# Three x tiles turned ahead of the key weights and one behind them, where it was two and two

## The chip, the core and the metric

The kernel runs on one core of a Trainium2 chip. The metric is device time in microseconds (us) of one execution, lower is better. A core has a matrix engine (PE, with its weight loads listed apart as PEld), a vector engine (DVE), a scalar engine (ACT), GpSimd (POOL) and SyncE (SP), which in this kernel only issues transfers. The transfers run on 16 DMA engines that all queues share.

## The reference

Two branches read the same input x (2048 tokens by 640, bf16) and are mixed by a gate for each token. In the first, x is multiplied by wqkv (640 by 1920) into queries, keys and values of 32 heads of 20. Queries and keys are multiplied by a small matrix w_phi of each head, and the features are the softmax of the result and the softmax of its negative. The state of a head is the sum over all tokens of (key features times values); an output is (query features times state) over a normaliser, and goes through wo. In the second branch the result is (gelu(x @ w_gate) * (x @ w_up)) @ w_down, with 1728 hidden columns. Cut to its core:

```python
phi_q = concatenate([softmax(q @ w_phi), softmax(-(q @ w_phi))])     # phi_k likewise
num = einsum("bhqf,bhfd->bhqd", phi_q, einsum("bhsf,bhsd->bhfd", phi_k, v))
den = einsum("bhqf,bhf->bhq", phi_q, phi_k.sum over tokens) + 1e-6
a = (num / den) @ wo
b = (gelu(x @ w_gate) * (x @ w_up)) @ w_down
g = sigmoid((x * gate_w).sum(-1))
out = g * a + (1 - g) * b
```

## The kernel before

The 2048 tokens are 16 tiles of 128. PE needs x with its columns on the partitions; that turned copy is `xT`, kept in SBUF for the whole kernel. Tiles 0 to 3 are loaded as they are (line 225) and turned by PE itself (line 331). Tiles 4 to 15 are turned on their way in by DMA transposes, each issued by `xturn(t, n)` (line 233) for n tiles from tile t on. One such DMA has one completion: whoever reads any of its n tiles waits for the whole of it.

Two more DMA transposes, issued by `wload` (line 229), bring the key part and the query part of wqkv in turned form: `wkT` and `wqT`, 640 by 640 each. They are needed because the kernel folds w_phi into the weights once: `fold(kt, "k", banks)` (matmuls on line 374, evictions on lines 383, 385 and 386) multiplies a block of `wkT` with a block-diagonal form of w_phi in a pair of PSUM banks, from where ACT or DVE copies one column of each head (`wref`) and DVE subtracts it from the others and writes the folded weight.

All transfers of the start are issued from SP's one queue, in the order of the code in `loads` (lines 242 to 251): two loads of x, five of the value weights, then the transposes. None of them waits for anything, so SP issues them one after another, and the DMA engines work them off in that order. The order of PE's work is the order of the code in `attention_state` (lines 539 to 612). Nothing is reordered: a helper, `_Sched`, only puts a wait on a semaphore ahead of an operation when something that it reads or overwrites isn't finished yet. Around the change it reads, with the PSUM banks as arguments:

```python
v(4, 6)
v(5, 0)
f(0, "k", (2, 3))
f(1, "k", (4, 5))
f(2, "k", (6, 7))
self.strip(6)
f(3, "k", (0, 1))
self.strip(0)
v(6, 2)
f(4, "k", (4, 5))
v(7, 6)
k(0, 0)
f(0, "q", (2, 3))
```

`v(t, b)` is ten matmuls (line 396, reached through `proj`) that project tile t on the value weights into banks b and b + 1, and an ACT eviction (line 437). It reads `xT` of tile t. `f` is a fold as above, six matmuls; `strip` is a small DVE memset of PSUM. `k` projects a tile on the folded key weights and takes exponentials on ACT (line 453).

After that a loop over the 16 tiles does keys, values, queries and the sum of the state (line 506), then the second branch runs for four blocks of 512 tokens (line 396 again, through `gateup`), and at the end the down projections with the output projection (line 717), their evictions (lines 728 and 730) and the stores.

Of the kernel before, what the change touches and what calls it, by code (L numbers as in the profile page):

```python
# [107 lines left out]
class _Kernel:  # L108
# [108 lines left out]
    def loads(self):  # L217
        sc, nc = self.sc, self.nc
        D, KD, DH, P_ = self.D, self.KD, self.DH, P
        w3 = self.wqkv.rearrange("(kt p) n -> p kt n", p=P)  # L220

        x4 = self.x[0:self.BT, :].rearrange("(p j) n -> p j n", j=self.TB)

        def xload(q, j):
            sc.dma(q, lambda e: e.dma_start(self.xtok[:, j:j + 2, :], x4[:, j:j + 2, :]),  # L225
                   writes=[("xtok", j), ("xtok", j + 1)])

        def wload(T, c0, key):
            sc.dma("sp", lambda e: e.dma_start_transpose(T[:, :, :], self.wqkv[:, c0:c0 + D]), writes=[key])  # L229

        def xturn(t, n):
            a, z = t * P, (t + n) * P
            sc.dma("sp", lambda e: e.dma_start_transpose(self.xT[:, :, a:z], self.x[a:z, :]),  # L233
                   writes=[("xT", k) for k in range(t, t + n)])
        sc.op("pool", lambda e: e.memset(self.gz[:, :], 0.0), writes=["gz"])
        sc.op("act", lambda e: e.activation(self.gtmp[:, 0:1], self.nc.const_aps.tensor(1.0, [P, 1], BF16), AF.Exp),
              writes=["gtmp"])
        sc.op("pool", lambda e: e.memset(self.ident[:, :], 0.0), writes=["ident"])
        sc.op("pool", lambda e: e.affine_select(self.ident[:, :], self.ident[:, :], pattern=[[-1, P]],
                                                compare_op=ALU.not_equal, fill=1.0, base=0, channel_multiplier=1),  # L240
              writes=["ident"])
        xload("sp", 0)
        xload("sp", 2)
        for kt in range(KD):
            sc.dma("sp", lambda e: e.dma_start(self.w3[:, kt, 0:D], w3[:, kt, 2 * D:3 * D]), writes=[("wv", kt)])  # L245
        xturn(4, 2)
        wload(self.wkT, D, "wkT")
        xturn(6, 2)
        wload(self.wqT, 0, "wqT")
        xturn(8, 4)  # L250
        xturn(12, 4)
        def pool(fn, writes, reads=()):
            sc.op("pool", fn, reads=reads, writes=writes)
        for i in range(KD):
            n = self.HHI[i] - self.HLO[i] + 1
            base = P * i - DH * self.HLO[i]
            m = self.mask[:, i, 0:n]
            pool(lambda e, m=m: e.memset(m, 1.0), [("mask", i)])
            pool(lambda e, m=m, n=n, base=base: e.affine_select(
                m, m, pattern=[[-DH, n]], compare_op=ALU.is_ge, fill=0.0, base=base, channel_multiplier=1),  # L260
                [("mask", i)])
            pool(lambda e, m=m, n=n, base=base: e.affine_select(
                m, m, pattern=[[DH, n]], compare_op=ALU.is_ge, fill=0.0, base=DH - 1 - base, channel_multiplier=-1),
                [("mask", i)])
        sc.dma("act", lambda e: e.dma_start(
            self.wphi_sb[:, :, :], self.wphi.rearrange("h d f -> (h d) f").rearrange("(i p) f -> p i f", p=P)),
            reads=[("mask", 1)], writes=["wphi"])
        sc.dma("act", lambda e: e.dma_start(self.gz[0:KD, :], self.gw.rearrange("(k p) -> k p", p=P)), writes=["gz"])
        for r in (0, 1):
            m = self.hmask[:, r, :]  # L270
            pool(lambda e, m=m: e.memset(m, 1.0), [("hmask", r)])
            pool(lambda e, m=m, r=r: e.affine_select(
                m, m, pattern=[[-DH, self.HG]], compare_op=ALU.is_ge, fill=0.0, base=-64 * r,
                channel_multiplier=1), [("hmask", r)])
            pool(lambda e, m=m, r=r: e.affine_select(
                m, m, pattern=[[DH, self.HG]], compare_op=ALU.is_ge, fill=0.0, base=DH - 1 + 64 * r,
                channel_multiplier=-1), [("hmask", r)])
        pool(lambda e: e.tensor_tensor(self.hmask[:, 2, :], self.hmask[:, 0, :], self.hmask[:, 1, :], ALU.add),
             ["hm"], reads=[("hmask", 0), ("hmask", 1)])
        for s in range(self.NSV):  # L280
            pool(lambda e, s=s: e.memset(self.vaug[:, s, :, DH:self.DA], 1.0), [("vone", s)])
        for s in range(self.NSE):
            pool(lambda e, s=s: e.memset(self.consts(self.Ek, s, 0), 1.0), [("Ekc", s)])
            pool(lambda e, s=s: e.memset(self.consts(self.Ek, s, 1), 1.0), [("Ekp", s)])
        for s in range(self.NEQ):
            pool(lambda e, s=s: e.memset(self.consts(self.Eqt, s, 0), 1.0), [("Eqtc", s)])
            pool(lambda e, s=s: e.memset(self.consts(self.Eqt, s, 1), 1.0), [("Eqtp", s)])
# [565 lines left out]
```

## Time and profile before

| | |
|---|---|
| median of 3 runs | 284.77 us (284.77 to 285.49) |
| the profiled execution's own time | 284.86 us |
| its span, first to last instruction | 283.5 us |
| PE busy | 280.3 us, 99% of the span |
| DVE, ACT, POOL busy | 172.8, 104.8, 13.2 us |
| granted clock of PE | 1.00 |
| moved by DMA | 24.11 MB, mean 85 GB/s |

Lines of an engine's order of time read: start, length, engine, line, operation, what is written and what is read, shapes, count, and in brackets the idle time before it with what ended it. "SPq" is SP's issue of a transfer, which ends long before the transfer does; the time from the start of an issue until the data are there is called landing. "q1" is the queue of the kernel's transfers, "q8" the one by which the engines fetch their instructions. GB/s stands in a strip of 40 equal slices of the stretch asked for. L396 is one helper line that serves most of the projections, so its rows are told apart by shape and by time.

### The profile page before, as it was taken

Reading aid. Unit: us, or ns where it says so; the run is one execution under the profiler, and the core shown is the slowest. Engines: PE = TensorE matmul, PEld = TensorE weight load, DVE = VectorE, ACT = ScalarE, POOL = GpSimd, SP = SyncE. Lnnn points to the kernel's source line nnn. Section 1 sums busy time; section 2 is a strip of 40 time slices with the busy share of each in tenths; the row PEclk is TensorE's granted clock in tenths of the full one; section 3 lists DMA queues with packets and bytes.
Section 4 is the critical chain, followed back from the end, with each engine's and each line's share of the span. In section 5 each row is a group of like instructions: output and inputs, shape, how many; then the busy total and the mean of one; then the engine's idle time right before and its main releaser. Section 6 shows DMA issues by size and latency. Waiting matters only on the chain.

```text
span 283.5 us, 6887 instructions
## 1 busy us (share of the span) xinstructions
PE 280.3 (99%) x2922; PEld 174.7 (62%) x2922; DVE 172.8 (61%) x325; ACT 104.8 (37%) x191; POOL 13.2 (5%) x67
## 2 busy tenths in 40 slices
PE   8999999999999999999999999999999999999996
PEld 5677777777754444444444444445777777777786
DVE  1369999999995332667242334325883883884801
ACT  4357888887852223222332223231112112012011
POOL 7500101110000000000000000000000000000000
DMA  8994398989999500011000000000133233232221
GB/s 227 189 219 91 60 198 179 192 180 165 171 250 353 146 0 0 2 23 24 2 0 0 0 2 0 0 0 2 25 50 85 58 44 76 72 44 76 73 73 49
DMA packets 58922, 24.11 MB, mean 85 GB/s; under 512 B 50954, under 2 KB 58378, under 8 KB 58890
## 3 DMA queue, kind: packets, MB, share of 16 engines
q1 hardware_dynamic: 58224, 23.63, 38.8%
q8 instruction: 23, 0.38, 0.6%
q10 hardware_dynamic: 666, 0.03, 0.2%
q14 instruction: 9, 0.07, 0.1%
HBM read 9.04 MB, written 2.62 MB: 41 GB/s over the span
## 4 chain that ended last, share of the span: by engine, by line
PE 94%; SPq 3%; DMA 2%; issue 0%; ACT 0%
PE ps L396 61%; PE ps L717 28%; PE ps L662 2%; DMA xT<-in_A_x_dram 2%; PE ps L506 2%; SPq L229 1%; SPq L245 1%; PE ps L374 1%; SPq L233 1%; SPq L225 0%; ACT outsb L730 0%
## 5 line engine op out<-in xcount | busy, mean ns | idle before, releaser
L396 PE MATMUL ps<-xT,wu_sb 128*128 128x512 bf16 x260 | 64.6, 379 | 0.0
L396 PE MATMUL ps<-xT,wg_sb 128*128 128x512 bf16 x260 | 64.6, 379 | 0.0
L633 ACT ACTIVATE gl<-ps 128x512 bf16<-128x512 f32 x52 | 31.1, 598 | 76.0 <-PE ps L396 73.8
L635 DVE TENSOR_TENSOR hT<-ps,gl 128x512 bf16<-128x512 f32 x39 | 26.7, 691 | 43.2 <-PE ps L396 43.2
L717 PE MATMUL ps<-wd_sb,hT 64*128 64x320 bf16 x648 | 48.4, 296 | 0.0
L396 PEld LDWEIGHTS ps<-xT,wu_sb 128*128 128x128 bf16 x260 | 25.4, 98 | 30.9 <-DVE hT L635 0.4
L396 PEld LDWEIGHTS ps<-xT,wg_sb 128*128 128x128 bf16 x260 | 25.0, 98 | 29.4
L730 ACT ACTIVATE outsb<-ps,Gm 128x320 bf16<-128x320 f32 (+2 forms) x31 | 14.6, 516 | 71.7 <-PE ps L717 71.7
L396 PE MATMUL ps<-w,xT 128*128 128x304 bf16 (+3 forms) x280 | 40.6, 296 | 0.3 <-DMA xT<-in_A_x_dram 0.3
L717 PEld LDWEIGHTS ps<-wd_sb,hT 64*128 64x128 bf16 x648 | 30.9, 94 | 12.2 <-issue 0.4
L396 PEld LDWEIGHTS ps<-w,xT 128*128 128x128 bf16 x280 | 26.4, 97 | 10.2 <-DMA xT<-in_A_x_dram 0.5
L717 PE MATMUL ps<-wo_sb,goT 64*128 64x320 bf16 (+2 forms) x340 | 26.5, 288 | 0.0
L495 DVE TENSOR_TENSOR Ek<-Ek,Dk 128x1320 bf16<-128x1320 bf16 x16 | 24.5, 1532 | 0.5
L688 DVE TENSOR_TENSOR O<-ps,RH 128x640 bf16<-128x640 f32 x32 | 24.8, 817 | 0.0
L486 DVE TENSOR_REDUCE Dk<-Ek 128x66 f32<-128x1320 bf16 x16 | 24.3, 1520 | 0.0
L396 PE MATMUL ps<-wq,xT 128*128 128x304 bf16 x160 | 23.3, 292 | 0.0
L453 ACT ACTIVATE Eqt<-ps 128x627 bf16<-128x627 f32 x32 | 20.5, 694 | 6.5 <-PE ps L396 6.5
L453 ACT ACTIVATE Ek<-ps 128x627 bf16<-128x627 f32 x32 | 20.5, 694 | 2.8 <-PE ps L396 2.6
L635 DVE TENSOR_TENSOR xT<-ps,gl 128x512 bf16<-128x512 f32 x13 | 9.0, 692 | 18.2 <-PE ps L396 18.2
L717 PEld LDWEIGHTS ps<-wo_sb,goT 64*128 64x128 bf16 x340 | 15.9, 94 | 5.3
L396 PEld LDWEIGHTS ps<-wq,xT 128*128 128x128 bf16 x160 | 15.0, 98 | 4.5
L717 PE MATMUL ps<-wd_sb,xT 64*128 64x320 bf16 (+2 forms) x270 | 16.0, 269 | 0.0
(77 smaller groups left out, 180.1 us busy)
## 6 DMA issues: line engine op xcount, KB each, us to landing
out_dram<-outsb SPq DMA_DIRECT2D x7, 320.0 KB, 2.3
wd_sb<-in_B_w_down_dram SPq DMA_DIRECT2D x1, 2080.0 KB, 10.6
wg_sb<-in_B_w_gate_dram SPq DMA_DIRECT2D x5, 224.0 KB, 4.0
wu_sb<-in_B_w_up_dram SPq DMA_DIRECT2D x5, 224.0 KB, 3.4
wg_sb<-in_B_w_gate_dram SPq DMA_DIRECT2D x5, 192.0 KB, 3.7
wu_sb<-in_B_w_up_dram SPq DMA_DIRECT2D x5, 192.0 KB, 3.3
w<-in_A_wqkv_dram SPq DMA_DIRECT2D x5, 160.0 KB, 4.0
wo_sb<-in_A_wo_dram SPq DMA_DIRECT2D x1, 800.0 KB, 9.6
```

What stands on the lines that cost most here:

```text
L229: sc.dma("sp", lambda e: e.dma_start_transpose(T[:, :, :], self.wqkv[:, c0:c0 + D]), writes=[key])
L396: self.sc.op("pe", lambda e: e.matmul(self.ps[:, bank * 512 + c0:bank * 512 + c0 + n], lhs, rhs, start=first, stop=fin), reads=reads, writ ...
L453: self.sc.op("act", lambda e: e.activation(dst, src, AF.Exp, scale=scale), reads=[("ps", b), ("ps", b + 1)], writes=[(name, sl, s)])
L486: self.sc.op("dve", lambda e: e.tensor_reduce(self.Dk[:, se, 0, :].rearrange("p (u h) -> p u h", h=self.HG), self.k_view(se), AX.X, ALU.ad ...
L495: sc.op("dve", lambda e: e.tensor_tensor(v, v, R.rearrange("p (u h) -> p u h", h=self.HG).unsqueeze(3).to_broadcast([P, 2 * self.G, self.H ...
L506: self.sc.op("pe", lambda e: e.matmul(self.bank(b)[:, c:c + n], self.Ek[:, se, g * P:(g + 1) * P], va[:, w * g:w * g + n], start=(t == 0 a ...
L633: sc.op("act", lambda e: e.activation(self.gl[:, slot, :], self.bank(banks[0]), AF.Gelu_apprx_tanh), reads=[("ps", banks[0])], writes=[("g ...
L635: sc.op("dve", lambda e: e.tensor_tensor(hT, self.bank(banks[1]), self.gl[:, slot, :], ALU.mult), reads=[("ps", banks[1]), ("gl", slot)], ...
L662: sc.op("pe", lambda e: e.matmul(self.ps[:, o:o + n], self.Eq[a:a + 64, g, t * P:(t + 1) * P], self.KV[a:a + 64, g, 0:n], start=(g in (0, ...
L688: dve(lambda e, o=o, f=f, s=s: e.tensor_tensor(o, V[s][:, :, 0:DH], f, ALU.mult), rb + [key(6 + s)], [("O", s, sl)], guard=old)
L717: sc.op("pe", lambda e: e.matmul(self.bank(bk, w), lhs, rhs, start=opens and x == 0, stop=end and not opens, skip_group_check=True), reads ...
L730: sc.op("act", lambda e: e.activation(dst, self.bank(bk, w), AF.Copy, scale=g), reads=rd, writes=wr)
```

## The change

The second x transpose gives one of its two tiles to the first. Tile 6 is turned by the DMA that is issued ahead of wkT, together with tiles 4 and 5; tile 7 alone is turned by the DMA between wkT and wqT. Nothing else differs: the number of transfers, the bytes, the order of the other entries in the queue and all instructions of the other engines are as before.

```diff
@@ loads
-        xturn(4, 2)
+        xturn(4, 3)
         wload(self.wkT, D, "wkT")
-        xturn(6, 2)
+        xturn(7, 1)
         wload(self.wqT, 0, "wqT")
         xturn(8, 4)
         xturn(12, 4)
```

## The prediction

> **What bounds the kernel now.** I read the page first, then the chain that ended last, then TensorE's (PE) order of time in the first 20 us, and last the queue of SP and the DMA by stretches. The page and the chain:
>
> ```profile
> span 283.5 us, 6887 instructions
> PE 280.3 (99%) x2922; PEld 174.7 (62%) x2922; DVE 172.8 (61%) x325; ACT 104.8 (37%) x191; POOL 13.2 (5%) x67
> ...
> PE 94%; SPq 3%; DMA 2%; issue 0%; ACT 0%
> ...
> 4.09 1.93 SPq L233
> 6.07 3.70 SPq L229
> 9.81 5.65 DMA xT<-in_A_x_dram
> 15.51 1.54 PE ps L396 x10
> ```
>
> PE is busy in 280.3 of 283.5 us. The chain runs through SP's queue until 9.81, through the transfer that turns tiles 6 and 7 until 15.46, and from 15.51 it is PE alone up to the last eviction. So whatever PE gains or loses near 15 us reaches the end whole, and nothing else here can. PE in that place, in order of time (start, length, idle in brackets):
>
> ```profile
> 11.00 2.90 PE L396 MATMUL ps<-w,xT 128*128 128x345 bf16 x20
> 13.74 1.50 PE L374 MATMUL ps<-BD,wkT 128*128 128x140 bf16 x24
> 15.51 1.54 PE L396 MATMUL ps<-w,xT 128*128 128x345 bf16 x10 [0.27 <-DMA xT<-in_A_x_dram]
> ...
> 13.61 1.44 PEld L374 LDWEIGHTS ps<-BD,wkT 128*128 128x128 bf16 x24
> ...
> 20.45 0.19 DVE L385 COPY wref<-ps 128x32 f32<-128x32 f32 x1 [1.53 <-PE ps L374]
> ```
>
> The first line is v of tiles 4 and 5 (they need the first turn, by the weight load at 10.94), the second the k folds 0 to 3 (they need wkT, from 13.61), the third v of tile 6, which sat 0.27 us for the second turn. These 0.27 us are all of PE's idle time between its start and its end. What SP issues and when it lands:
>
> ```profile
> 4.09 1.93 SPq L233 DMA_TRANSPOSE xT<-in_A_x_dram  x1
> 9.81 1.40 SPq L233 DMA_TRANSPOSE xT<-in_A_x_dram  x1
> 11.26 4.77 SPq L229 DMA_TRANSPOSE wqT<-in_A_wqkv_dram  x1
> ...
> DMA to landing us min/median/max: 4.8/4.8/4.8
> DMA to landing us min/median/max: 6.5/6.5/6.5
> DMA to landing us min/median/max: 7.8/7.8/7.8
> ```
>
> The landings are those of the first turn, of wkT and of wqT: 4.09 + 4.8 = 8.9, 6.07 + 6.5 = 12.6, 11.26 + 7.8 = 19.1. Slack before use: 10.94 - 8.9 = 2.0 for tiles 4 and 5, 13.61 - 12.6 = 1.0 for wkT, 19.74 (first weight load on wqT) - 19.1 = 0.65 for wqT; tile 6 has -0.27. The DMA between 12.8 and 14.6 us:
>
> ```profile
> GB/s 637 267 290 267 256 40 0 0 0 0 0 0 0 0 0 0 0 0 0 0 6 6 6 11 6 11 6 11 6 11 11 6 11 11 6 11 6 17 23 245
> q8 instruction: 1, 0.02, 3.3%
> ```
>
> One fetch of 16 KB of instructions starts there (12.8), and from 13.0 to 14.55 all 16 DMA engines stand nearly still: the second x turn was in flight, and it landed at 15.46 only. The next ones begin at 24.3, 37.1, 49.7 and 62.9, at PE's pace, so the first comes at 12.8 in the changed kernel too, as PE has done the same by then.
>
> **The change part by part.** Instructions on PE, DVE, ACT and POOL are the same in number and order; only two entries of SP's queue change size. The number of DMA issues stays.
>
> First turn, two tiles to three. A tile is 128 x 640 x 2 B = 164 KB. In full flow the DMA moves 288 GB/s (its mean from 14.6 to 17.4 us), so one tile is 0.57 us. Landing 8.9 + 0.57 = 9.5, use at 10.94: hidden, by v of tiles 0 to 3 on PE. SP's issue grows from 1.93 by between 0.2 (a 128-token turn in the output stage issues in 1.20, a 256-token one in 1.40) and 1.0 a tile (512 tokens take 3.45 at the end of this series, (3.45 - 1.40)/2). I take 0.6, the middle, near the DMA's own 0.57.
>
> wkT, moved behind one more tile. It lands 0.2 to 1.0 later by the issue, 0.57 later by the flow: 12.8 to 13.6, taken as 13.15. Use at 13.61: slack 0.45 where it was 1.0, and at the far end of the bound none. Behind it on PE stand all folds and everything else, in order.
>
> Second turn, two tiles to one. It ends as early as before or earlier, since the bytes ahead of it are the same: 15.46 at the latest by the flow. Tile 7 is first wanted when v of tile 6 (10 matmuls, 1.54) and fold 4 (0.32) are done, 17.2: hidden by 1.7 us. SP's issue of it costs 1.20 to 1.40, so wqT's issue begins at 11.0 to 11.9 instead of 11.26; its bytes ahead are the same, so 19.1 is kept, against a use that comes 0.1 sooner (19.6). The later turns (8 to 15) follow wqT and have several us.
>
> Tile 6 then is there at 9.5, and PE's wait of 0.27 goes. What is late next: v of tile 6 writes banks 2 and 3, which fold 0 used; they come free when DVE has evicted them:
>
> ```profile
> 14.55 0.80 DVE L386 TENSOR_TENSOR w<-ps,wref 128x608 bf16<-128x608 f32 x1
> ```
>
> That is 15.35, and with the 0.05 that the chain shows between a release and PE's start, 15.40. So PE starts v of tile 6 at 15.40 and not at 15.24, where the folds ahead of it end: the gain is 15.51 - 15.40 = 0.11, with 0.27 as the upper bound. After that DVE and ACT follow PE: fold 4 and tile 7 need evictions that end at 16.1 and 16.9, before 17.0, and the q folds' evictions start only when PE has written (DVE's line at 20.45 above waits for PE), so they move along.
>
> Sum: 284.86 (the profiled execution: span 283.5 and 1.36 around it) - 0.11 = 284.75, beside a median of 284.77; the profiled execution stands 0.09 above that median.
>
> **The skill against the row.** The Trainium skill's page "DMA: Bandwidth & Descriptors", section "Latency and other measured facts", gives 261 GB/s for DMA transposes whose middle dimension isn't contiguous. By that a tile would take 0.63 instead of 0.57, wkT would land 0.06 later still, and the sum would be the same. The same page's "Queues, rings and completion order" says that an engine's completion write lands only after all its earlier writes, those of other queues among them. By that rule an instruction fetch that is served before wkT's last write on one engine would hold the whole of wkT back, which speaks against the change; the trace shows only the standstill of 1.55 us in an x turn, and no landing of wkT behind a fetch. The sum by that rule would be the first rival's, by the row alone 284.75.
>
> **The rivals.** *The fetch catches wkT (slower).* Before, wkT is in at 12.6, ahead of the fetch at 12.8; after, it is due at 12.8 to 13.6, inside the standstill. If a part of it is still on the way at 13.0, it comes when the DMA moves again, 14.55, or up to 15.46 as the x turn did. PE would idle from 13.74 to W + 0.05, DVE's evictions move with it, and 0.11 is still won: 14.55 gives 0.86 - 0.11 = +0.75, 15.46 gives 1.77 - 0.11 = +1.66: 285.6 to 286.5, middle 286.05. It decides from a landing of 13.8 on. For it: the two times meet. Against: wkT's reads would be done by about 11.15 + 0.57 = 11.7 (in 8.05 to 11.15 the flow is even, then it breaks to 16 GB/s), a full us before the fetch, and only completions would be open.
>
> *wkT a little late.* Landing between 13.7 and 14.5 for the far end of SP's issue or a longer completion: -0.1 to +0.7, some 285.1. wqT shows a tail as long: its reads end at 17.4 and it lands at 19.1, 1.7 later where wkT's tail is 1.4.
>
> *Three tiles in one turn land late.* A 512-token turn takes 6.5 to 7.1 from issue to landing; 4.09 + 7.1 = 11.2 would hold tile 4 by 0.25, and push wkT to 14.8, +1.0: 285.9. Against it: that turn starts behind wqT's tail and holds four tiles.
>
> *Nothing is won.* DVE's eviction or another wait in its place takes all of 0.27: 284.86.
>
> **How the numbers follow.** Chances: the gain of 0.11, 0.43; the fetch catches wkT 0.36; a little late 0.12; three tiles late 0.05; nothing or something else 0.04. A measurement of this kernel can tell about 0.3%, 0.85 us, from no change: the limits are 283.9 and 285.6. Faster than 283.9 isn't to be had from 0.27 us of idle time: 0.03. Slower takes nearly all of the fetch's case (0.35), most of the late tiles (0.03) and a rest: 0.39. Within: 0.58. The likeliest case's own range is 284.5 to 285.2; the range with the rivals is 284.4 to 286.4, which leaves out the tails of both.
>
> **What would show it.** Right: no idle time of PE before v of tile 6 for a DMA, a short one at most for DVE's eviction; wkT's landing from its issue such that the folds start at 13.74 as before; tile 6 landed by 10. Wrong: PE or its weight loads idle before the first fold (L374) with wkT as releaser, and the length of that idle time less 0.1 is then the loss. If DMA stands still elsewhere than at 13.0, the fetch has moved, and the second rival falls. Most likely to make the prediction wrong is the size of wkT's delay: 0.45 us of slack are worked out from a flow, not seen.

## The result and the profile after

The changed kernel takes 286.02 us in the median of 16 runs (285.39 to 287.14), the kernel before 285.23 in 16 runs taken beside them (284.59 to 285.51): a ratio of 1.0031, 95% interval 1.0021 to 1.0041. It is slower by 0.8 us. The profiled execution took 286.26 us, 1.40 more than that of the kernel before. Single executions scatter by about 1 us, so traces are compared with traces and medians with medians.

The page of the changed kernel, and from its chain that ended last (start, length, what) the pieces around the change:

```profile
span 284.9 us, 6886 instructions
PE 280.6 (98%) x2922; PEld 174.5 (61%) x2922; DVE 172.7 (61%) x325; ACT 104.8 (37%) x191; POOL 13.2 (5%) x67
...
PE 94%; DMA 3%; SPq 2%; DVE 0%; issue 0%; ACT 0%; DVEq 0%
```

```profile
4.09 3.09 SPq L233
7.24 7.94 DMA wkT<-in_A_wqkv_dram
15.22 0.50 PE ps L374 x6
16.04 0.81 DVE w L386
16.90 1.54 PE ps L396 x10
```

PE is busy as long as before, so what was lost is idle time. The chain no longer goes through the turn of tile 6 but through wkT: its issue begins at 7.24 where it was 6.07, and it lands 7.94 later, at 15.18, where it was 12.57. PE in order of time:

```profile
11.80 2.91 PE L396 MATMUL ps<-w,xT 128*128 128x345 bf16 x20 [0.55 <-DMA xT<-in_A_x_dram]
15.22 1.43 PE L374 MATMUL ps<-BD,wkT 128*128 128x140 bf16 x24 [0.51 <-DMA wkT<-in_A_wqkv_dram]
16.90 1.54 PE L396 MATMUL ps<-w,xT 128*128 128x345 bf16 x10 [0.24 <-DVE w L386]
```

Three waits stand where there was one. Tiles 4 and 5 wait for the first turn, which takes 7.7 us to land instead of 4.8 (4.09 + 7.7 = 11.8):

```profile
DMA to landing us min/median/max: 7.7/7.7/7.7
```

The folds wait for wkT. Then v of tile 6 waits, no more for a transfer but for DVE's eviction of fold 0. It starts at 16.90 against 15.51, 1.39 later, and this is the whole of the 1.40 us.

Why both transfers are late is seen in the DMA from 8.7 to 12 us (GB/s in 40 slices of 0.0825 us). First the kernel before, then the changed one:

```profile
GB/s 43 270 289 292 292 289 292 285 292 292 289 292 295 279 298 289 292 292 289 292 285 289 295 289 292 289 285 292 295 197 59 25 40 22 59 81 93 112 143 177
```

```profile
GB/s 267 143 68 65 115 99 71 47 47 71 90 130 121 99 304 93 74 96 74 22 19 19 12 0 0 0 9 6 9 9 9 9 9 9 12 34 261 295 292 276
...
q8 instruction: 1, 0.02, 1.8%
```

Before, wkT is read without a break at some 290 GB/s until 11.1, and no instructions are fetched meanwhile; the first fetch starts at 12.8, behind it. After, the flow is thin at the same place, some 50 to 140 GB/s from 8.8 on. At 9.9 the instruction fetch starts (the lone 304), and from 10.3 to 11.6 nearly nothing moves. A transpose reads its data in packets of 256 B, so that counting them tells which transfer is being read: the 1,920 packets of the first turn are read by 8.85, so the thin flow behind it is wkT's own start. wkT's reads end near 14.0 instead of 11.1.

### The profile page after: what moved, and what is told of

Its sections match the earlier page's. It is cut to its first block, busy times and chain, and to the rows that moved or that the text cites. A ratio compares the mean times of both kernels' runs of the same rounds, so it can differ in the third digit from the quotient of the medians.

```text
span 284.9 us, 6886 instructions
## 1 busy us (share of the span) xinstructions
PE 280.6 (98%) x2922; PEld 174.5 (61%) x2922; DVE 172.7 (61%) x325; ACT 104.8 (37%) x191; POOL 13.2 (5%) x67
## 4 chain that ended last, share of the span: by engine, by line
PE 94%; DMA 3%; SPq 2%; DVE 0%; issue 0%; ACT 0%; DVEq 0%
PE ps L396 60%; PE ps L717 28%; DMA wkT<-in_A_wqkv_dram 3%; PE ps L662 2%; PE ps L506 2%; SPq L233 1%; PE ps L374 1%; SPq L245 1%; SPq L225 0%; DVE w L386 0%; ACT outsb L730 0%; DVE wref L385 0%; DVEq L42 0%
## 5 line engine op out<-in xcount | busy, mean ns | idle before, releaser
L730 ACT ACTIVATE outsb<-ps,Gm 128x320 bf16<-128x320 f32 (+2 forms) x31 | 14.6, 516 | 71.8 <-PE ps L717 71.8
L717 PEld LDWEIGHTS ps<-wo_sb,goT 64*128 64x128 bf16 x340 | 15.9, 94 | 5.3
## 6 DMA issues: line engine op xcount, KB each, us to landing
wd_sb<-in_B_w_down_dram SPq DMA_DIRECT2D x1, 2080.0 KB, 11.3
```

What stands on the lines that cost most here:

```text
L717: sc.op("pe", lambda e: e.matmul(self.bank(bk, w), lhs, rhs, start=opens and x == 0, stop=end and not opens, skip_group_check=True), reads ...
L730: sc.op("act", lambda e: e.activation(dst, self.bank(bk, w), AF.Copy, scale=g), reads=rd, writes=wr)
```

## The experiments

Four explanations were held against each other. The *size theory*: a turn of three tiles has a long tail of its own. The *bytes theory*: wkT is late by the 164 KB ahead of it and by no more. The *issue* (or *starvation*) *theory*: SP is held by the longer first turn, wkT's issue begins too late, and its reads run thin. The *fetch theory* was added to the last: PE's instruction fetch, which gets in when the flow is thin, halts the transposes. In the recorded expectations of the first runs it is a part of the issue theory.

### Tiny loads on SP ahead of wkT (e1_sp_delay)

```diff
         xturn(4, 2)
+        for i in range(3):
+            sc.dma("sp", lambda e: e.dma_start(self.tiny[:, i, :], self.gw.rearrange("(p k) -> p k", p=P)), writes=[("tiny", i)])
         wload(self.wkT, D, "wkT")
```

> The kernel before, with three loads of a few bytes on SP's queue between the first turn (tiles 4 and 5) and wkT: each costs SP about 0.43 us of issue, the order and the bytes of all else stay. Issue theory (the third tile hurts because SP is occupied by the first turn for 3.09 us instead of 1.93, so wkT's issue begins at 7.24 instead of 6.07, the DMA engines run out of issued work near 8.7, and an instruction fetch then gets in at 9.9 and halts the transposes): wkT's issue begins near 7.4, the flow of 288 GB/s breaks between 8 and 9.5, the fetch comes near 10 instead of 12.8, wkT lands between 14 and 15.3, PE sits before the first fold for 0.4 to 1.7 us, and the time is 0.5 to 1.6 us above the kernel before. Size theory (a turn of three tiles has a long tail of its own) and bytes theory (wkT is late because 164 KB more stand ahead of it): neither size nor bytes change, wkT lands by 13, the time stays within 0.3 us of the kernel before.

Measured: 286.51 us, ratio 1.0059 (1.0046 to 1.0071). wkT's issue begins at 8.21. The DMA from 8.2 to 10.6 us, and PE's only large wait (line 377 is line 374 of the kernel before):

```profile
GB/s 286 286 294 178 55 42 26 7 2 2 3 2 2 5 7 3 0 0 0 0 0 0 60 85 107 107 128 145 149 158 145 154 196 183 243 222 213 213 128 107
```

```profile
15.49 1.43 PE L377 MATMUL ps<-BD,wkT 128*128 128x140 bf16 x24 [1.54 <-DMA wkT<-in_A_wqkv_dram]
```

No turn has grown, and three times 128 packets of 10 B, under 4 KB in all, are no load: the DMA engines stand mostly idle from 8.5 to 9.5. Yet wkT lands at 8.21 + 7.2 = 15.4. Size and bytes theory both fall as the whole cause: a late issue alone makes the DMA run dry and then run thin. The fetch came at 13.2, not near 10 as expected, and hit the end of wkT: a second place where it does harm. How much of the 1.54 us it makes, and how much the late issue, this run doesn't separate.

### The same tiles ahead of wkT in two transfers (e3_split)

```diff
-        xturn(4, 3)
+        xturn(4, 2)
+        xturn(6, 1)
         wload(self.wkT, D, "wkT")
         xturn(7, 1)
```

> The changed kernel with its first turn in two transfers, tiles 4 and 5, then tile 6, both ahead of wkT. Same bytes in the same order, but no transfer of three tiles. Issue theory: SP needs 1.9 + 1.2 = 3.1 us for the two, wkT's issue begins near 7.3 as in the changed kernel, the flow breaks and the fetch comes near 10; wkT lands between 14 and 15.3; tile 4 no longer waits (landing near 9), so PE sits only before the folds, for 0.4 to 1.7 us: 0.3 to 1.5 us above the kernel before. Size theory: the tail goes with the size, wkT lands by 13.3, the time is 0 to 0.3 us below the kernel before.

Measured: 285.90 us, ratio 1.0033 (1.0020 to 1.0046), as much as the change itself. SP is busy with the two turns from 4.11 to 7.97, and wkT's issue begins at 8.01. PE:

```profile
14.85 1.43 PE L375 MATMUL ps<-BD,wkT 128*128 128x140 bf16 x24 [0.87 <-DMA wkT<-in_A_wqkv_dram]
16.61 1.53 PE L397 MATMUL ps<-w,xT 128*128 128x345 bf16 x10 [0.33 <-DVE w L387]
```

The wait of tile 4 is gone with the long transfer, the wait for wkT is not, and the time doesn't fall. So the size theory explains at most the wait of tile 4, and this wait isn't needed for the loss. What size alone costs wkT the run doesn't price, because its issue begins 0.77 us later than in the changed kernel (8.01 against 7.24).

### All four tiles ahead of wkT (e6_four)

```diff
-        xturn(4, 3)
+        xturn(4, 4)
         wload(self.wkT, D, "wkT")
-        xturn(7, 1)
```

> The changed kernel with tile 7 in the first turn as well: four tiles ahead of wkT, none behind it. Starvation theory: SP's issue of the first turn lasts until the DMA has read all but some 1400 of its 2560 packets, to 8 or later, so wkT's issue begins at 8.2 or later, its reads at 9.5 or later, and it lands between 14 and 16.5: 0.4 to 2.5 us above the kernel before. Bytes theory: wkT is late by the 328 KB that are new ahead of it, 1.14 us at 288 GB/s: it lands at 13.7, and the time is within 0.3 us of the kernel before.

Measured: 286.50 us, ratio 1.0048 (1.0035 to 1.0061). SP's issue of the turn takes 4.49 us, wkT's begins at 8.63 and it lands at 15.7:

```profile
12.22 2.91 PE L395 MATMUL ps<-w,xT 128*128 128x345 bf16 x20 [1.33 <-DMA xT<-in_A_x_dram]
15.73 1.43 PE L373 MATMUL ps<-BD,wkT 128*128 128x140 bf16 x24 [0.60 <-DMA wkT<-in_A_wqkv_dram]
```

The issue grows with every tile (1.9, 3.1, 4.5 us for two, three, four). The loss is 0.48% where the change's is 0.31%, but their intervals overlap, so that it grows is not shown. The bytes theory, within 0.3 us, fails again.

### Value weights issued from ACT (e2_act_loads, and its control e7_before_act)

```diff
-            sc.dma("sp", lambda e: e.dma_start(self.w3[:, kt, 0:D], ...
+            sc.dma("sp" if kt < 3 else "act", lambda e: e.dma_start(self.w3[:, kt, 0:D], ...
```

> The changed kernel (three tiles, then one), with the last two of the five value-weight loads issued from ACT's queue instead of SP's: SP reaches the first turn 0.9 us earlier, its size and the bytes stay. Issue theory: first turn issued from 3.2, wkT from about 6.3, the DMA still has work issued ahead when the first turn is done, the flow holds to the end of wkT, the fetch comes after it, wkT lands by 13.3, tile 4 by 9.8, PE doesn't sit before the folds, and the time is 0.9 to 1.5 us below the changed kernel in its profile, 0 to 0.3 us below the kernel before. Size theory: the tail of the first turn stays (landing at 11 or later), wkT lands at 14 or later, the time stays 0.5 us or more above the kernel before.

> The kernel before with the last two value-weight loads issued from ACT's queue. It is the control for the changed kernel with the same edit: what the edit alone does. Issue theory: SP is 0.9 us ahead, wkT lands at 12.6 or up to 0.5 earlier, the fetch still falls behind wkT into the second turn, tile 6 still waits for it up to 15.4: within 0.3 us of the kernel before. If the value weights themselves come later from ACT's queue, v of tiles 0 to 3 would stretch, and this run shows it: tiles 4 and 5 would start after 11.0.

Measured: 287.40 us, ratio 1.0082 (1.0069 to 1.0096) with three tiles first, 285.92 us, 1.0033 (1.0020 to 1.0045) with two. The edit does harm by itself: loads from two queues share the DMA, the first x tiles come later, and PE starts its transposes 0.7 us (two tiles) or 1.1 us (three) later. As a remedy it says nothing. Held against each other, the third tile costs 1.5 us here, but not by way of wkT: with three tiles first PE waits neither for tile 4 nor for wkT, and the difference stands already at the start of v of tile 4 (13.78 against 12.09). SP's queue with three tiles first shows something else:

```profile
3.15 4.17 SPq L233 DMA_TRANSPOSE xT<-in_A_x_dram  x1
7.37 3.93 SPq L229 DMA_TRANSPOSE wkT<-in_A_wqkv_dram  x1
```

SP reaches the first turn 0.94 us sooner than in the changed kernel, but is held in it until 7.32 where that one was done at 7.18. So the issue of a three-tile turn isn't so many us of SP's work: something else ends it. With two tiles SP took 1.76 from the same start, so it wasn't held. The packets tell what it may be. When SP's issue of a turn of three tiles ended, 1,560, 1,478 and 1,528 of its 1,920 packets were still unread in the three traces of the changed kernel, 1,569 here and 1,414 in e10_early90_after; of four tiles it was 1,524 of 2,560 in e6_four. Two tiles are 1,280 packets, fewer than that. So SP seems to be held until some 1,400 to 1,600 packets are left to read. No run was made to test this, and it stays an inference from six traces.

### Moving the fetch a little (e5_fetch_after, e8_fetch_before)

```diff
-        for n in (512, 512, 512, 512, 512, 512, 128, 128, 128):
+        for n in (512,) * 3 + (32,) * 40:
```

> The changed kernel with PE's nine warm-up matmuls at the start (6 of 512 columns, 3 of 128) replaced by 43 (3 of 512, 40 of 32): 34 more matmuls, so that PE's first instruction fetch, which came at 9.9 us, is asked for near 5, while plain loads run. The warm-up's results are not used. Fetch theory (the standstill from 10.0 to 11.55 that the fetch makes is what holds wkT back): the standstill is gone, the first turn lands by 10.3, wkT by 13.7, PE sits 0.2 us at most before v of tile 4 and before the folds, and the time is within 0.4 us of the kernel before. Starvation theory (wkT is late because SP's issue runs only a limited amount ahead of the DMA, so that wkT's start runs thin after a first turn of three tiles, whatever the fetch does): flow still thin from 8.75 to 10 or longer, wkT lands at 14 or later, PE sits 0.4 us or more before the folds, and the time stays 0.4 to 1.0 us above the kernel before.

> The kernel before with the same warm-up of 43 matmuls: the control for the run above. Fetch theory: the standstill from 13.0 to 14.55 goes, the second turn lands by 14.2, PE waits for DVE's eviction alone, and the time is 0 to 0.25 us below the kernel before. If the fetch among the plain loads delays the value weights, or the shorter warm-up slows PE, the time rises, and v of tile 4 begins after 11.1; then the run with the changed kernel is to be held against this one.

Measured: 285.69 us, ratio 1.0029 (1.0016 to 1.0043) for the changed kernel, 286.19 us, 1.0038 (1.0023 to 1.0052) for the control. The fetch didn't come near 5 but at 9.1 and at 7.9, so neither run is free of a fetch among the transposes, and the control is slower than the kernel before where a gain was expected. In these runs the change costs nothing: the changed kernel isn't slower than its control with the same warm-up. The control's trace is evidence for the fetch all the same. Its SP queue is that of the kernel before (first turn from 4.11 for 1.88, wkT from 6.03); the warm-up is another, and the fetch has moved from 12.8 to 7.9. The DMA from 7.8 to 9.8 us, and PE's wait behind it:

```profile
GB/s 297 594 282 266 282 256 287 261 287 261 206 72 20 15 20 15 0 0 0 0 0 0 0 5 10 10 5 10 5 10 10 10 10 5 15 5 10 10 10 5
...
q8 instruction: 1, 0.02, 3.5%
```

```profile
16.09 1.54 PE L396 MATMUL ps<-w,xT 128*128 128x345 bf16 x10 [0.67 <-DMA xT<-in_A_x_dram]
```

After 0.5 us the DMA stands nearly still for 1.4 us. The first turn lands at 4.11 + 6.4 = 10.5 (8.9 before) and wkT at 6.03 + 7.9 = 13.9 (12.6 before). With issue, size and bytes as they were, wkT has moved by 1.3 us with the fetch. (Beside the second trace of the kernel before, below, it is 0.5.) In the changed kernel with this warm-up wkT lands at 7.63 + 7.4 = 15.0 and PE waits 0.66 us for it, as the starvation theory has it; but with a fetch at 9.1 that doesn't decide against the fetch theory.

### Moving the fetch ahead of the transposes (e10_early90_after, e11_early90_before)

```diff
-        for n in (512, 512, 512, 512, 512, 512, 128, 128, 128):
+        for n in (32,) * 90 + (512,) * 2:
```

> The changed kernel with a warm-up of 90 matmuls of 32 columns and 2 of 512 in place of the 9, so that PE's first instruction fetch is asked for at about 3.5 us, ahead of all transposes; the second one then falls near 15. Fetch theory: no standstill between 6 and 14; the flow may be thin from 8.7 to 10, but the first turn lands by 10.3, wkT by 13.7, and PE sits 0.2 us at most before the folds. Starvation theory: the thin flow alone costs as much; wkT lands at 14 or later, PE sits 0.4 us or more. Nothing is read from the total, as the second fetch now falls into wqT.

> The kernel before with the same warm-up of 92 matmuls, the control. Both theories: no standstill from 6 to 14, wkT lands at 12.6 or earlier, the second turn by 14.2 instead of 15.5. If wkT lands later than 12.9 here, the warm-up itself disturbs the loads, and the run above is to be held against this one.

Now the first fetch starts at 5.6 and 5.7 us, and none falls between 6 and 17. Measured: 285.55 us, ratio 1.0021 (1.0012 to 1.0030) for the changed kernel, 285.38 us, 1.0015 (1.0006 to 1.0024) for the control: the two lie within each other's intervals, though the totals settle nothing, as in both the second fetch falls at 17.8, into wqT. The order of time of the changed kernel, and wkT's landing from its issue, in it (issue at 7.93) and in the control (issue at 6.18), each with v of tile 6:

```profile
14.12 1.44 PE L374 MATMUL ps<-BD,wkT 128*128 128x140 bf16 x24 [0.28 <-DMA wkT<-in_A_wqkv_dram]
15.80 1.54 PE L396 MATMUL ps<-w,xT 128*128 128x345 bf16 x10 [0.24 <-DVE w L386]
...
DMA to landing us min/median/max: 6.1/6.1/6.1
```

```profile
15.71 1.53 PE L396 MATMUL ps<-w,xT 128*128 128x345 bf16 x10 [0.25 <-DMA xT<-in_A_x_dram]
...
DMA to landing us min/median/max: 7.1/7.1/7.1
```

wkT lands at 14.0 against 13.3 in the control: with no fetch in wkT's way the third tile costs it 0.7 us, where the two plain traces differ by 2.6. And v of tile 6 starts at 15.80 against 15.71, so of the 1.39 us there 0.09 is left. Neither theory's number is met: the fetch theory wanted 13.7 and at most 0.2 of waiting, the starvation theory 0.4. The control, too, lands wkT 0.4 later than it was held to: the start of its first turn is thin (14 to 47 GB/s from 7.1 to 8.4), for which the early fetch may be the cause. So without a fetch in wkT's way the late issue and the thin start cost little at v of tile 6; the change's loss there came with a fetch inside wkT's reads.

### wkT in two transfers (e12_wksplit_before, e13_wksplit_after)

```diff
-        wload(self.wkT, D, "wkT")
+        for r0, r1, key in ((0, 2 * P, "wkTa"), (2 * P, D, "wkTb")):
+            sc.dma("sp", lambda e: e.dma_start_transpose(self.wkT[:, :, r0:r1], self.wqkv[r0:r1, D:2 * D]), writes=[key])
...
-                    reads=["w%sT" % which, ("BD", i)], writes=[("ps", b)], signal=fin)
+                    reads=["wqT" if which == "q" else "wkTa" if kt < 2 else "wkTb", ("BD", i)], writes=[("ps", b)], signal=fin)
```

> The kernel before with wkT brought by two transposes, rows 0 to 255 and then 256 to 639, each with its own completion; folds 0 and 1 need the first, folds 2 to 4 the second. Fetch theory: folds 0 and 1 have their data by 10.5, folds 2 to 4 by 13.2 at a standstill elsewhere or by 14.5 at one in it; PE wants fold 2 at 14.4. No wait before fold 0, at most 0.1 before fold 2: within 0.25 us of the kernel before in its median. One more issue on SP (some 0.1 to 1.2 us) moves the second turn and wqT: if wqT comes after 19.7, up to 0.5 us above.

> The changed kernel with wkT brought by the same two transposes. If the loss comes through the whole of wkT landing late (both theories), the first part lands by 12.6 even with the standstill at 10 to 11.55, folds 0 and 1 start on time, and only folds 2 to 4 wait for the rest, which lands near 15.2 and is wanted at 14.4: the loss falls by 0.4 to 0.7 us to 0.2 to 0.7 above the kernel before. If the wait of tile 4 for the first turn is as large as in the changed kernel's profile (0.55), it stays.

Measured: 284.98 us, ratio 1.0012 (0.9998 to 1.0026) on the kernel before, not told from it; 285.17 us, 1.0011 (1.0003 to 1.0020) on the changed one. So two thirds of the change's loss go when folds 0 and 1 needn't wait for the whole of wkT, and the two kernels with this edit, 0.2 us apart, aren't told from each other. PE in the changed kernel with this edit:

```profile
13.74 1.67 PE L375 MATMUL ps<-BD,wkT 128*128 128x140 bf16 x24
15.40 1.54 PE L397 MATMUL ps<-w,xT 128*128 128x345 bf16 x10
...
20.32 0.80 PE L375 MATMUL ps<-BD,wqT 128*128 128x140 bf16 x12 [0.40 <-DMA wqT<-in_A_wqkv_dram]
```

The folds start at 13.74 as in the kernel before, and v of tile 6 at 15.40, the very time that the prediction worked out; what is left of the loss is now wqT's, which comes 0.40 too late. The fetch stood at 8.8 here, at the end of the first turn's reads, and wkT's second part landed at 14.6 only. This shows that the loss runs through wkT.

### Tile 6 and tile 7 apart, behind wkT (e9_six_seven)

```diff
-        xturn(6, 2)
+        xturn(6, 1)
+        xturn(7, 1)
```

> The kernel before with its second turn in two transfers, tile 6 and tile 7, both behind wkT. What is ahead of wkT is untouched. Both theories: wkT lands at 12.6 as before. Tile 6's 640 packets of 256 B are read by about 12.5, ahead of the fetch at 12.8: if its completion gets out by 13.0 tile 6 lands before 14 and PE's wait of 0.27 shrinks to DVE's 0.16, 0 to 0.25 us below the kernel before; if the fetch catches it, it lands near 15.2 and the time is that of the kernel before, within 0.3.

Measured: 285.55 us, ratio 1.0019 (1.0007 to 1.0030): a little slower, not faster. SP needs 3.47 us for the two turns instead of 1.40, wqT's issue begins at 13.61 instead of 11.26, and its folds wait 0.15. The fetch started at 11.34, and wkT landed at 13.6, not 12.6, though nothing ahead of it had changed; the second trace of the kernel before, below, has the same pair, 11.2 and 13.4.

### Two more traces of each kernel (look_after1, look_after2, look_before1, look_before2)

> The changed kernel as it is, another execution with its trace. Fetch theory: the instruction fetch starts between 8.5 and 10.5, before wkT's reads are done, the DMA stands nearly still for about 1.5 us after it, wkT lands at 14 or later, and PE sits 0.4 us or more before the folds. If in this execution the fetch comes after 11.5 and wkT still lands at 14 or later, the fetch is not what holds wkT back; if the fetch comes late and wkT lands by 13.7, the theory holds and the place of the fetch is chance.

> The changed kernel once more, as in the first of these looks: fetch between 8.5 and 10.5, wkT at 14 or later.

> The kernel before as it is, another execution with its trace. Fetch theory: the fetch starts at 11 or later, at the end of wkT's reads or behind it, wkT lands by 13.7, PE sits 0.1 us at most before the folds. If the fetch comes by 10 here too and wkT still lands by 13, the theory falls.

> The kernel before once more: fetch at 11 or later, wkT by 13.7.

| trace | us | wkT issue from | fetch at | wkT lands | PE waits for tile 4, for wkT |
|---|---|---|---|---|---|
| before | 284.86 | 6.07 | 12.8 | 12.6 | 0, 0 |
| look_before1 | 285.18 | 6.01 | 11.2 | 13.4 | 0, 0 |
| after | 286.26 | 7.24 | 9.9 | 15.2 | 0.55, 0.51 |
| look_after1 | 286.58 | 7.19 | 11.3 | 15.6 | 0, 1.13 |
| look_after2 | 285.84 | 7.12 | 9.5 | 14.9 | 0.19, 0.62 |

The fetch itself isn't bound to 9 or 10: in look_after1 it came at 11.3, outside the time expected. What is the same in all three traces of the changed kernel is that it falls before wkT's reads are done, and that these start thin. The DMA of look_after1 from 8.6 to 10 us shows the thin start without any fetch, and the DMA from 11 to 13.2 us and its PE row what it came to with the fetch behind it:

```profile
GB/s 307 278 236 133 117 95 66 51 66 102 103 110 154 110 110 73 66 95 88 95 117 146 110 161 154 183 146 168 190 117 132 73 88 66 66 95 110 102 73 168
```

```profile
GB/s 172 289 289 279 289 568 279 270 256 33 0 0 0 0 0 0 0 0 0 0 0 0 9 9 5 9 9 9 9 9 9 9 9 9 9 9 33 275 289 289
...
q8 instruction: 1, 0.02, 2.7%
```

```profile
15.66 1.43 PE L375 MATMUL ps<-BD,wkT 128*128 128x140 bf16 x24 [1.13 <-DMA wkT<-in_A_wqkv_dram]
```

In before and look_before1 wkT's reads run at full flow and are done at 11.1, and the fetch comes at that time or after. look_before1 also shows what the fetch costs when it comes right at the end: wkT lands 0.9 us later than in the other trace, 13.4, still in time, as PE wants it at 13.6 in the other trace and at 14.1 in this one:

```profile
14.20 1.50 PE L375 MATMUL ps<-BD,wkT 128*128 128x140 bf16 x24
...
DMA to landing us min/median/max: 7.4/7.4/7.4
```

look_before1 and look_after1 are the clearest pair of all, as the fetch comes at nearly the same time, 11.2 and 11.3. In the first 99% of wkT's packets are read by then and wkT lands at 13.4; in the second 42% are, and it lands at 15.6. Over the pairs of runs with the same edit the third tile delays wkT by 0.7 us with no fetch in the way (13.3 to 14.0), by 1.1 with fetches at 7.9 and 9.1 (13.9 to 15.0) and by 2.2 in this one.

A thin flow isn't needed for the fetch to get in. In e12_wksplit_before and e13_wksplit_after it started at 9.1 and 8.8 out of a flow of 280 GB/s, and in look_after1 too. In ten of the sixteen traces whose first fetch falls among the transposes it started within 0.2 us of the end of one transpose's reads (10.04 in e6_four, whose four tiles are read by 10.05), in the other six, before and after among them, in the middle of one. What sets its time is open.

The fourth trace, look_before2, took 289.73 us at a mean granted clock of 0.994, and it isn't like the others: the DMA stands still from 9.4 to 10.6 with no fetch, and again after a fetch at 11.3; wkT lands at 15.9. One of 35 runs of the kernel before, 289.0, was as long. What makes the first of these standstills is open, and its expectation (wkT by 13.7) was missed.

## Why the prediction was wrong

The forecast was 284.75 with a chance of 0.58 for no difference; measured is 286.02, slower, and with a ratio of 1.0031 right at the 0.3% that the prediction had set as its bound. The time lies in the range, near the middle of the first rival. Some of that is luck: the kernel before itself had a median of 285.23 in the 16 runs beside it, 0.46 above the 284.77 that the forecast started from.

*PE alone sets the end:* right. The 1.39 us at v of tile 6 are the 1.40 at the end.

*"So it comes at 12.8 in the changed kernel too":* this is the step that failed. The fetch came at 9.9, 11.3 and 9.5 in the changed kernel, and at 12.8 and 11.2 in the one before. One trace had shown one time, and the prediction took it as fixed by PE's progress. PE's progress does move it, as the longer warm-ups show, but with one and the same warm-up it came anywhere from 8.8 to 13.2 over the traces of all edits. With the fetch moved to 7.9, wkT came 1.3 us later in the kernel before; with it out of the way the third tile's delay was 0.7 us.

*wkT lands at 12.8 to 13.6:* wrong, 15.2, 15.6 and 14.9. Without a fetch in the way the delay was sized right: 0.7 measured against the 0.2 to 1.0 that it was bounded by. Missing was the standstill inside its reads, and the thin start, which leaves more of wkT unread when the fetch comes: with the fetch at 11.2 and 11.3 the delay was 2.2.

*SP's issue grows by 0.6:* too small. It grew by 1.16 (1.93 to 3.09), beyond even the far bound of 1.0. The bound took the issue for so many us of SP's work for each tile; in the pair with loads from ACT three tiles took 4.17, so it isn't.

*Tile 4 is hidden at 9.5:* wrong in two of three traces. The first turn landed at 11.8, 10.1 and 11.3, and tile 4 waited 0.55, 0 and 0.19. The rival "three tiles in one turn land late" had the place, at 0.05; in the trace with the longest wait the fetch fell between the end of this turn's reads, 8.85, and its landing.

*DVE's eviction takes the place of tile 6's wait:* right. PE waits 0.24 for line 386 in all three traces (0.16 was worked out), and in the run with wkT in two transfers v of tile 6 starts at 15.40 as forecast.

*The first rival, the fetch catches wkT:* its price, 285.6 to 286.5, was right; its way was not. It had the fetch at 12.8 meet the last completions of wkT. In the traces it falls into wkT's reads. The argument against it, reads done by 11.7, was the flow's even rate once more: they end between 13.6 and 14.5. Between 0.43 and 0.36 the wrong one was put first because the time of the fetch was believed from a single execution.

*The rule of the skill:* the Trainium skill, "DMA: Bandwidth & Descriptors", section "Queues, rings and completion order", has a completion wait for all earlier writes of its engine, other queues included. look_before1 doesn't contradict it: with the fetch at 11.2, as wkT's reads end, wkT's landing is 13.4 against 12.6. But the flow is thin on all engines in that time too, so no run here tells the rule from the halt of the flow. The row of a halted transpose, which was in the first trace, and the rule spoke against the change together, and were worth more weight than they got.

## What to carry to other kernels

Whether the queue keeps the DMA fed can matter more than the bytes in it: before a transfer is made longer, look at when the next one's issue begins and whether the flow in between stays full. A standstill in a trace that comes from something asynchronous, such as an instruction fetch, has a place only in that execution: price the change with it at every place where it could fall, and take more than one trace before relying on a slack below its length. Where one late transfer holds a chain of small users, splitting its completion can be worth more than reordering: it took back two thirds of the loss here, though it made the kernel before no faster.

## What the runs showed of the hardware

A fetch of 16 KB of instructions that started in the middle of a transpose's reads was followed by a halt on all 16 engines: in the kernel before from 13.0 to 14.55, in the changed one from 10.3 to 11.6, in the control run e8_fetch_before from 8.4 to 9.8, 1.3 to 1.55 us each for a packet that itself took 0.9 to 1.1 us. One that started as a transpose's reads ended, as in e6_four at 10.04, was followed by a thin flow, 10 to 175 GB/s until 11.85. look_before2 has a like halt without a fetch, so a fetch may not be its only cause.

SP's issue of a transpose isn't a fixed time: three tiles took 3.09 us from 4.09 and 4.17 us from 3.15, ending at 7.18 and 7.32. As a first turn, two tiles took 1.76 to 2.5 us.

A transpose whose issue begins late starts thin: wkT in the changed kernel, whose issue had begun 1.6 us before its forerunner's reads ended, ran at some 50 to 140 GB/s for about a us. wkT in the kernel before, issued 2.15 us before that point (6.07 and 8.22), ran at 290 GB/s from its first packets but for a dip at 8.7. In the other traces it started thin with 1.7 us or less, and full with 1.8 us or more.
